# From the ninth pair on, DMA transposes the third row block's probabilities as planes of half words; x and residual pages share one ring

## The chip, the cores and the metric

The kernel runs on one core of a Trainium2 chip. The metric is device time in microseconds of one launch. Engines: TensorE (PE, with weight loads listed as PEld), VectorE (DVE), ScalarE (ACT), GpSimd (POOL), and SyncE (SP), which issues almost all DMAs. Each engine runs its instructions in the order of its own queue; semaphores hold an instruction until what it reads has been written and what it overwrites has been read.

## The reference

Two stages. Attention, with B = 8, H = 8, S = 576, D = 64, masked by blocks of 64 positions; then a gated MLP on x, the attention output laid out as (B, S, 512):

```python
scores = scale * np.matmul(q, k.transpose(0, 1, 3, 2))
mask = block_i >= block_j                     # blocks of 64 positions
scores = np.where(mask, scores, -1000000000.0)
attn = np.exp(scores - np.max(scores, axis=-1, keepdims=True))
attn = attn / (np.sum(attn, axis=-1, keepdims=True) + 1e-09)
x = np.matmul(attn, v)                        # (B, H, S, D), then to (B, S, H*D)

h = gelu_tanh(x @ w_in)                       # 512 -> 1024
u, v = h[..., :512], h[..., 512:]
v_n = (v - mean(v)) / np.sqrt(var(v) + 1e-06) * g_ln
v_s = np.einsum('ts,bsd->btd', w_sg, v_n) + b_sg[None, :, None]
out = x + (u * v_s) @ w_out
```

All tensors are float32.

## The kernel before

**Work and slots.** A pair is one batch and two heads; there are 32, four to a batch. The main loop runs one *slot* for each pair n. It finishes pair n (transposes of its probabilities, product with v, normalisation) and makes the scores and probabilities of pair n+1; in the *holes* between these steps PE gets pieces of the MLP of an earlier batch. Slots 0 to 3 are `opening_slot`, 4 to 7 `middle_slot`, 8 to 31 `slot`. The pieces come from `work` in the order v, u, o of the batch before, s, so that the four slots of a batch differ: from slot 8 on the first has mostly v pieces (x @ w_in for the v half, `accv`), the second u pieces (`accu`), the third the eight o pieces (w_out and the residual sum, `acco`) along with the LayerNorm of v, the fourth s pieces (spatial product and gate, `accs`). They are called the v, u, o and s slot; slots 8 and 12 are v slots, 10 and 14 o slots.

**Precision.** A float32 product is made of three matmuls of split operands, hi and lo (`xh`, `xl`, `kh`, `kl`, ...). The transposes of the probabilities and their product with v are plain float32.

**One slot in order** (`slot`). Loads of v and of q, k for later pairs; `turn("A0")`, `turn("A1")`: four 128 x 128 transposes each by PE into a PSUM bank, copied to an SBUF page `pt`; holes; `turn("B0")`, `turn("B1")`; holes; `turn("C")`: the four blocks of the third row block `prob_119`, two of each head, copied by DVE into `ptC`; `turn_sums` (`pd`); holes; `Scores.first` of the next pair (scores `s`, masked maximum on DVE, exponent on ACT); `products` (`ob`, which reads all `pt` pages); `normalise`, which writes the page x and spills it to DRAM; `Scores.second`, whose last part is the third row block; `Values.inverse`, from pair 4 on `spread`: sums and their reciprocal on DVE, the 32 x 32 block transpose `rt`, a DMA of it to DRAM (`rows`), and two DMAs that spread the rows over the partitions (`rb`); `split_qk` on POOL; holes, with LayerNorm work of DVE in between. So the end of `rt` on DVE marks the end of a slot's attention work.

**What sets the order.** Through slot 7 all engines keep program order. From slot 8 on only PE does (`written.intersection_update("P")`); the instructions of DVE, ACT, POOL and SP are put in order by a scheduler when the program is built. Two kinds of DVE work keep their program order all the same: `bn_stats` (L659) and the centring (L665).

**Pages.** `pt` has five buffers, shared by `ptA`, `ptB`, `ptC`, the last part of v (`vt`) and, up to slot 10, the conversion of w_out (`tm`). The page x has a ring of two buffers ("x"), the residual `xr` another ring of two ("r"): the o pieces load a spilled x into `xr`, add `acco` to it, and store it to `out_T`. The tag `rx` serves only pairs 0 to 3.

The lines that the change and the prediction touch:

```python
KINDS = {"x": ("x", 2), "xr": ("r", 2), "xh": ("y", 5), "xl": ("z", 5)}
TE = {"A0": "a", "A1": "v", "B0": "a", "B1": "v", "C": "v"}
"C": [(0, 2, 0), (0, 2, 1), (1, 2, 0), (1, 2, 1)],     # head, row block, column block
```

Of the kernel before, what the change touches and what calls it, by code (L numbers as in the profile page):

```python
# [9 lines left out]
F32 = mybir.dt.float32  # L10
F32R = mybir.dt.float32r
BF16 = mybir.dt.bfloat16
U32 = mybir.dt.uint32
AF = mybir.ActivationFunctionType
ALU = mybir.AluOpType
# [5 lines left out]
def kernel(  # L21
# [14 lines left out]
    P = 128  # L36
    BLK = 64
# [24 lines left out]
    vector = Engine("V", nc.vector)  # L62
    scalar = Engine("A", nc.scalar)
    gpsimd = Engine("G", nc.gpsimd)
    tensor = Engine("P", nc.tensor)
    sync = Engine("S", nc.sync)

    cp = ctx.enter_context(tc.tile_pool(name="cp", bufs=1))
    sp = ctx.enter_context(tc.tile_pool(name="sp", bufs=1))
    dp = ctx.enter_context(tc.tile_pool(name="dp", bufs=2, space=DRAM))  # L70
    psum = ctx.enter_context(tc.tile_pool(name="psum", bufs=1, space=PSUM))

    KINDS = {"x": ("x", 2), "xr": ("r", 2), "xh": ("y", 5), "xl": ("z", 5)}
    KINDS.update({n: ("a", 9) for n in ("vv", "vh", "vl")})
    KINDS.update({n: ("b", 12) for n in ("u", "gh", "gl", "w")})

    def page(dtype, n, name):
        tag, bufs = KINDS.get(name, KINDS["w"])
        return sp.tile([P, n], dtype, tag=tag, name=name, bufs=bufs)

    def bank(name):
        return psum.tile([P, 512], F32, tag="bank", name=name, bufs=8)
# [10 lines left out]
    def copy(e, dst, src):  # L93
        f = {"v": vector.tensor_copy, "a": scalar.copy, "g": gpsimd.tensor_copy}[e]
        return f(dst, src)
# [28 lines left out]
    def split_qk(n):  # L124
        out = []
        for x, t in zip(raw.pop(n), "qk"):
            hi = sp.tile([P, S], F32R, tag=t + "h", name=t + "h", bufs=1)
            lo = sp.tile([P, S], F32R, tag=t + "l", name=t + "l", bufs=1)
            if n:
                copy("g", hi, x)  # L130
                behind["G"] = gpsimd.tensor_tensor(lo, x, hi.bitcast(F32), op=ALU.subtract)
            out += [hi, lo]
        qk[n] = out
# [47 lines left out]
    MW = EXT[NT - 2]  # L181
    mask = cp.tile([P, MW], BF16, name="mask")
    gpsimd.memset(mask, 0.0)
# [12 lines left out]
    for s in (0, 1):  # L196
        t = cp.tile([P, NT - 1, 2 * D], F32, name=f"v_f{s}")
        d = cp.tile([P, NT, 2 * D], F32, name=f"v_d{s}")
        for a in (0, 1):
            r = slice(a * D, (a + 1) * D)  # L200
# [4 lines left out]
    prob = [[pairs[i][:, a * EXT[i] : (a + 1) * EXT[i]] for i in range(NT)] for a in (0, 1)]  # L205
# [39 lines left out]
    def load_weight(src, off, cols, dh, dl, name, size):  # L245

        parts = [(c, f) for f in range(0, cols, W) for c in range(NC)]
        for k in range(0, len(parts), size):
# [9 lines left out]
            if src.dtype == F32:  # L258
# [5 lines left out]
                continue  # L264
            words = [x.bitcast(U32).rearrange("p (n t) -> p n t", t=2) for x in raw]
            if size == 2:
                m = page(U32, size * W, name)
            else:
                tm = sp.tile([P, 2 * W], U32, tag="pt", name="tm", bufs=5)
                t, m = tm[:, :W], tm[:, W:]  # L270
# [8 lines left out]
            if size == 2:  # L279
                t = page(U32, size * W, name)  # L280
                y = bank("w").bitcast(U32)
            else:
# [180 lines left out]
    Q = H // 2  # L463
# [9 lines left out]
    class Values:  # L473
# [20 lines left out]
        def inverse(self):  # L494
# [9 lines left out]
                r.unsqueeze(2).broadcast_to([P, NT * 2, D]),  # L504
            )

        def spread(self):

            r = sums32[:, : 2 * NT]
            vector.tensor_scalar_add(  # L510
                r.rearrange("p (a i) -> p a i", a=2), self.sm.rearrange("p i a -> p a i"), 1e-9
            )
            vector.reciprocal(r, r)
            rt = sp.tile([P, 32], F32, tag="rt", name="rt", bufs=1)
            vector.transpose(rt, sums32)
            rows32 = dp.tile([32, P], F32, tag="rows", name="rows", bufs=2)
            sync.dma_start(rows32.rearrange("c (g p) -> g c p", g=P // 32), rt)
            while between:
                between.popleft()()
            rows = rows32[: 2 * NT, :].rearrange("(a i) p -> a (i p)", a=2)  # L520
            self.d = sp.tile([P, NT * BLK + S], F32, tag="rb", name="rb", bufs=1)
            rb = self.d[:, NT * BLK :]
            for a in (0, 1):
                sync.dma_start(
                    rb[a * D : (a + 1) * D, :], rows[a : a + 1, :S].broadcast_to([D, S])
                )
            self.rb = rb[:, : S - BLK]
            self.r0 = rb[:, S - BLK :]
# [68 lines left out]
    def run_side(k):  # L597

        while k > 0 and side and side[0][0] != "G":
            k -= 1  # L600
            side.popleft()[1]()
# [187 lines left out]
    def hole(k=1):  # L789

        while k > 0 and work:
            try:
                next(work[0])
                k -= 1
            except StopIteration:
                work.popleft()
# [64 lines left out]
    def slot(n, va):  # L861
        nx = n + 1 < N
        k = 3
        g = [int(x) for x in (FIRST if n // Q == 1 else PLAN)[n % Q]]
        if n + 1 < N:
            load_v(n + 1)
        if n + 2 < N:
            load_qk(n + 2)
        va.turn("A0")
        va.turn("A1")  # L870
        hole(g[0])
        run_side(k)
        split_pending()
        load_share(n, 0)
        va.turn("B0")
        va.turn("B1")
        hole(g[1])
        run_side(k)
        va.turn("C")
        va.turn_sums()  # L880
        hole(g[2])
        run_gelu()
        load_share(n, 1)
        if nx:
            nx = Scores(n + 1)
            nx.first()
        va.products()
        va.normalise()
        if nx:
            nx.second()  # L890
        load_share(n, 2)
        if n % Q == Q - 1:
            va.split()
        else:
            pending.append(va.split)
        nv = None
        if nx:
            nv = Values(n + 1, nx)
            nv.inverse()
        if n + 2 < N:  # L900
            split_qk(n + 2)
        load_share(n, 3)
        for _ in range(g[3]):
            hole()
            run_side(k)
        return nx, nv
# [55 lines left out]
    def middle_slot(n, va):  # L962

        script = SCRIPT[n]
        g = [int(x) for x in FIRST[n % Q]]
        load_qk(n + 2)
        load_v(n + 1)
        va.turn("A0")
        va.turn("A1")
        if n != 2 * Q - 2:  # L970
            split_pending()
        run_gelu()
        hole(g[0])
        script[0]()
        va.turn("B0")
        va.turn("B1")
        hole(g[1])
        script[1]()
        va.turn("C")
        va.turn_sums()  # L980
        hole(g[2])
        script[2]()
        nx = Scores(n + 1)
        nx.first()
        va.products()
        va.normalise()
        nx.second()
        if n % Q == Q - 1:
            va.split()
        else:  # L990
            pending.append(va.split)
        script[3]()
        nv = Values(n + 1, nx)
        nv.inverse()
        split_qk(n + 2)
        script[4]()
        hole(g[3])
        script[5]()
        return nx, nv
# [14 lines left out]
    va = Values(0, sc)  # L1014
    for n in range(N):
        if n == 2 * Q:
            written.intersection_update("P")
        sc, va = (opening_slot, middle_slot, slot)[min(n // Q, 2)](n, va)
# [51 lines left out]
```

## Time and profile before

| what | value |
|---|---|
| median of 3 runs | 735.6 us (735.31 to 735.82) |
| the profiled execution | 736.18 us, span 734.1 us, mean granted clock 0.997 |
| PE busy | 721.1 us (98%) in 6796 matmuls |
| DVE busy | 481.0 us (66%) |
| ACT busy | 397.6 us (54%) |
| POOL busy | 301.2 us (41%) |
| DMA | 78.75 MB, 107 GB/s over the span |
| `pC`, 128 transposes | 20.2 us busy, pipelined |
| `ptC` by DVE, 24 copies | 16.5 us busy |

Busy times are of one execution. A line such as "DVE ... x32 | 13.6, 468 | 0.6" reads: 32 instructions, 13.6 us together, 468 ns each, and 0.6 us in which the engine stood idle just before them, with what ended the wait. In a timeline the two numbers ahead are the start and the duration in us, and the bracket is the idle time before and its releaser. Matmuls overlap, so what a block of them holds of PE is the distance between starts. "SPq" is SP issuing a DMA; the duration is that of the issue, not of the transfer.

### The profile page before, as it was taken

Reading aid. Unit: us, or ns where it says so; the run is one execution under the profiler, and the core shown is the slowest. Engines: PE = TensorE matmul, PEld = TensorE weight load, DVE = VectorE, ACT = ScalarE, POOL = GpSimd, SP = SyncE. Lnnn points to the kernel's source line nnn. Section 1 sums busy time; section 2 is a strip of 40 time slices with the busy share of each in tenths; the row PEclk is TensorE's granted clock in tenths of the full one; section 3 lists DMA queues with packets and bytes.
Section 4 is the critical chain, followed back from the end, with each engine's and each line's share of the span. In section 5 each row is a group of like instructions: output and inputs, shape, how many; then the busy total and the mean of one; then the engine's idle time right before and its main releaser. Section 6 shows DMA issues by size and latency. Waiting matters only on the chain.

```text
span 734.1 us, 18266 instructions
## 1 busy us (share of the span) xinstructions
PE 721.1 (98%) x6796; PEld 674.9 (92%) x6796; DVE 481.0 (66%) x1489; ACT 397.6 (54%) x1021; POOL 301.2 (41%) x333
## 2 busy tenths in 40 slices
PE   8999989999999999999999999999999999999998
PEld 7888979899998999989999899998999989998997
DVE  6988976569864487635876459654696456841732
ACT  6996768287533854347543575346663376602500
POOL 5868844555341253522445223453234433321120
PEclk9999999999999999999999999999999999999999
DMA  5667434354441225322263133531336322230032
GB/s 165 186 170 224 122 106 132 90 144 125 123 138 59 82 88 166 111 68 74 87 186 106 41 89 100 168 93 41 91 99 169 90 64 83 83 98 1 17 114 97
DMA packets 92907, 78.75 MB, mean 107 GB/s; under 512 B 64530, under 2 KB 65170, under 8 KB 92820
## 3 DMA queue, kind: packets, MB, share of 16 engines
q1 hardware_dynamic: 92532, 77.30, 35.8%
q8 instruction: 54, 0.88, 0.5%
q14 instruction: 33, 0.27, 0.1%
q10 hardware_dynamic: 288, 0.30, 0.1%
HBM read 58.23 MB, written 19.33 MB: 106 GB/s over the span
## 4 chain that ended last, share of the span: by engine, by line
PE 71%; DVE 15%; ACT 5%; POOL 4%; issue 3%; DMA 0%; SPq 0%; DVEq 0%; ACTq 0%; POOLq 0%
PE accs L60 16%; PE accv L60 14%; PE acco L60 9%; PE s L60 8%; PE ob L60 8%; PE accu L60 7%; ACT prob L60 4%; POOL rs L60 3%; DVE prob L60 3%; DVE bs L659 3%; PE pB L60 2%; PE pA L60 2%; DVE vl L60 2%; PE pd L60 2%; PE pC L60 1%
## 5 line engine op out<-in xcount | busy, mean ns | idle before, releaser
L60 ACT ACTIVATE prob<-prob,negm 128x576 f32<-128x576 f32 (+3 forms) x320 | 176.4, 553 | 58.0 <-DVE negm L60 56.6
L60 DVE CUSTOM_DVE_ANT_0 prob<-s,mask 128x256 f32<-128x256 f32 (+3 forms) x320 | 119.4, 417 | 36.8 <-PE s L60 33.9
L60 POOL TENSOR_TENSOR xh<-x,xh 128x64 fp32r<-128x64 f32 x32 | 10.3, 323 | 195.7 <-DVE xh L60 114.0
L60 POOL TENSOR_TENSOR gl<-u,gh 128x288 fp32r<-128x288 f32 x64 | 52.0, 818 | 86.0 <-DVE gh L60 65.9
L60 PE MATMUL acco<-gh,wo_h 128*128 128x288 f32 x256 | 77.3, 302 | 3.2 <-DVE negm L60 3.2
L60 PE MATMUL accu<-xh,wi_h 128*128 128x288 f32 x256 | 78.6, 307 | 0.0
L60 PE MATMUL accs<-ws_h,vh 128*128 128x288 f32 x256 | 77.9, 304 | 0.0
L60 PE MATMUL accu<-xh,wi_l 128*128 128x288 f32 x256 | 75.9, 296 | 0.0
L60 PE MATMUL accu<-xl,wi_h 128*128 128x288 f32 x256 | 75.8, 296 | 0.0
L60 PE MATMUL acco<-gh,wo_l 128*128 128x288 f32 x256 | 75.4, 295 | 0.0
L60 PE MATMUL accs<-ws_l,vh 128*128 128x288 f32 x256 | 75.4, 295 | 0.0
L60 PE MATMUL accs<-ws_h,vl 128*128 128x288 f32 x256 | 75.4, 294 | 0.0
L60 PE MATMUL acco<-gl,wo_h 128*128 128x288 f32 x256 | 75.3, 294 | 0.0
L60 PE MATMUL s<-kh,qh 64*128 64x320 f32 (+4 forms) x384 | 66.2, 325 | 3.2 <-DVE negm L60 2.7
L60 PE MATMUL accv<-wi_h,xh 128*128 128x512 f32 x160 | 65.5, 410 | 0.0
L60 DVE TENSOR_TENSOR u<-accs,u 128x288 f32<-128x288 f32 x64 | 29.2, 456 | 52.5 <-PE accs L60 50.0
L60 PE MATMUL accv<-wi_l,xh 128*128 128x512 f32 x160 | 63.1, 394 | 0.0
L60 PE MATMUL s<-kh,ql 64*128 64x320 f32 (+4 forms) x384 | 60.7, 304 | 0.0
L60 ACT ACTIVATION_READ_ACCUMULATOR prob<-prob,negm 128x1 f32 x320 | 60.0, 187 | 0.0
L60 PE MATMUL s<-kl,qh 64*128 64x320 f32 (+4 forms) x384 | 58.9, 301 | 0.0
L60 ACT COPY vv<-accv 128x512 f32<-128x512 f32 x32 | 18.6, 582 | 68.3 <-PE accv L60 68.3
L60 PEld LDWEIGHTS s<-kh,qh 64*128 64x128 f32 x384 | 38.3, 187 | 15.6 <-issue 9.1
(123 smaller groups left out, 2025.8 us busy)
## 6 DMA issues: line engine op xcount, KB each, us to landing
spill<-x SPq DMA_DIRECT2D x32, 288.0 KB
xr<-spill SPq DMA_DIRECT2D x32, 288.0 KB
out_T<-xr SPq DMA_DIRECT2D x32, 288.0 KB
q_f<-in_qT SPq DMA_DIRECT2D x31, 288.0 KB
k_f<-in_kT SPq DMA_DIRECT2D x31, 288.0 KB
rb<-rows SPq DMA_DIRECT2D x56, 144.0 KB
v_f<-in_v SPq DMA_DIRECT2D x32, 128.0 KB
v_d<-in_v SPq DMA_DIRECT2D x64, 64.0 KB
```

What stands on the lines that cost most here:

```text
L60: return lambda *a, **k: pin(method(*a, **k), self.letter)
L659: tc.keep_in_program_order(nc.vector.bn_stats(bs[:rows, :], x))
```

## The change

For pairs 8 to 31 the four PE transposes of `turn("C")` and DVE's copy out of PSUM go. In their place the new method `flip`, called right behind `inverse` in `slot` (for pair 8 in slot 7), views the float32 probabilities as pairs of half words: two POOL copies, one for each head, sort them into a plane of low and a plane of high half words (`halves`, 128 x 1024 of 16 bits, 256 KB); one transposing DMA on SP's queue turns its eight 128 x 128 blocks (`flipped`); one DVE copy of 1024 half words per partition joins the planes into float32 again, in `ptC`. The page x and the residual get one common ring of three buffers in place of two rings of two. Pairs 0 to 7 keep `turn("C")`.

```diff
-    KINDS = {"x": ("x", 2), "xr": ("r", 2), "xh": ("y", 5), "xl": ("z", 5)}
+    KINDS = {"x": ("x", 3), "xr": ("x", 3), "xh": ("y", 5), "xl": ("z", 5)}
...
+        def flip(self):
+
+            i = 2
+            halves = sp.tile([P, 2 * 2 * i * P], U16, tag="rx", name="halves", bufs=1)
+            sides = halves.rearrange("p (t a n) -> p t a n", t=2, a=2)
+            for a in (0, 1):
+                x = prob[a][i][:, a * BLK : a * BLK + i * P].bitcast(U16)
+                gpsimd.tensor_copy(sides[:, :, a, :], x.rearrange("p (n t) -> p t n", t=2))
+            flipped = sp.tile([P, 2 * 2 * i * P], U16, tag="flipped", name="flipped", bufs=1)
+            sync.dma_start_transpose(flipped.rearrange("p (m q) -> p m q", q=P), halves)
+            pt = sp.tile([P, 512], F32, tag="pt", name="ptC", bufs=5)
+            vector.tensor_copy(
+                pt.bitcast(U16).rearrange("p (n t) -> p t n", t=2),
+                flipped.rearrange("p (t n) -> p t n", t=2),
+            )
+            for a in (0, 1):
+                for j in range(i):
+                    c = (a * i + (i - 1 - j if a else j)) * P
+                    self.pt[a, i, j] = pt[:, c : c + P]
+
...
@@ slot
-        va.turn("C")
         va.turn_sums()
...
             nv.inverse()
+            nv.flip()
...
@@ middle_slot
         nv.inverse()
         split_qk(n + 2)
+        if n == 2 * Q - 1:
+            nv.flip()
```

On PE the order is otherwise the same. On DVE and SP the scheduler puts the work of a slot in another order. DVE at the start of slot 14, an o slot (530 us in the trace of before; `bs`, `stats` and `vv` are LayerNorm, `pA` and `pB` the PSUM banks of the transposes), before:

```order
L60 STREAM_TRANSPOSE rt<-sums_99 128x32
L659 BN_STATS bs<-vv 128x6
L60 BN_AGGR stats<-bs 128x2
L659 BN_STATS bs<-vv 128x6
L60 BN_AGGR stats<-bs 128x2
L659 BN_STATS bs<-vv 128x6
L60 CAST xh<-x 128x576
L60 BN_AGGR stats<-bs 128x2
L659 BN_STATS bs<-vv 128x6
L60 BN_AGGR stats<-bs 128x2
L659 BN_STATS bs<-vv 64x6
L60 COPY ptA_4146<-pA_4145 128x512
```

and with the change:

```order
L61 STREAM_TRANSPOSE rt<-sums_99 128x32
L61 CAST xh<-x 128x576
L61 TENSOR_TENSOR xr<-acco,xr 128x288 x2
L61 COPY ptC<-flipped 128x2x512
L680 BN_STATS bs<-vv 128x6
L61 COPY ptA_4153<-pA_4152 128x512
L61 COPY ptB_4216<-pB_4215 128x512
L61 TENSOR_TENSOR xr<-acco,xr 128x288
L61 BN_AGGR stats<-bs 128x2
L680 BN_STATS bs<-vv 128x6
```

The copy of `flipped` stands fourth, ahead of all five moments, of `ptA` and of `ptB`; before, `ptC` stood behind `ptB` and the centring. Two residual sums moved ahead of the moments. In v and u slots the copy stands directly behind `rt` with nothing between, in s slots behind two or three pairs of gate products (`u<-accs`, `gh<-u`).

SP at the same place, before (`xr_4152` and `xr_4168` are the first two residual pages of the o slot, loaded some twelve issues or more ahead of this):

```order
L60 DMA spill_4001<-x_3998 128x576
L60 DMA v_f1_113<-in_v 64x4x64 x2
L60 DMA v_d1_114<-in_v 64x4x64
L60 DMA rows_4031<-rt_4029 4x32x32
L60 DMA rb_4033<-rows_4031 64x576 x2
L60 DMA k_f_4135<-in_kT 128x576
L60 DMA q_f_4134<-in_qT 128x576
L60 DMA out_T<-xr_4152 128x576
L60 DMA xr_4388<-spill_1846 128x576
L60 DMA out_T<-xr_4168 128x576
```

and with the change:

```order
L61 DMA spill_4001<-x_3998 128x576
L61 DMA v_f1_113<-in_v 64x4x64 x2
L61 DMA v_d1_114<-in_v 64x4x64
L61 DMA xr_4159<-spill_1281 128x576
L61 DMA xr_4175<-spill_1577 128x576
L61 DMA rows_4031<-rt_4029 4x32x32
L61 DMA rb_4033<-rows_4031 64x576 x2
L61 DMA k_f_4142<-in_kT 128x576
L61 DMA_TRANSPOSE flipped_4039<-halves_4036 128x8x128
L61 DMA q_f_4141<-in_qT 128x576
L61 DMA out_T<-xr_4159 128x576
L61 DMA out_T<-xr_4175 128x576
```

The transpose stands behind `rows`, both `rb` and the load of k; in v and u slots it stands right behind `rb`. The two residual loads that ran far ahead are now issued just before `rows`, since the common ring has no buffer for them earlier.

More of the change, by code (lines that the diff above doesn't have):

```diff
@@ L12 @@
 BF16 = mybir.dt.bfloat16
+U16 = mybir.dt.uint16
 U32 = mybir.dt.uint32
```

## Prediction

> **What bounds the kernel now.** I read the busy times first, then the chain of waits that ended last, then the stretches between the ends of neighbouring `rt` transposes on VectorE (DVE), because that instruction closes a slot and the new copy is put right behind it.
>
> ```profile
> span 734.1 us, 18266 instructions
> PE 721.1 (98%) x6796; PEld 674.9 (92%) x6796; DVE 481.0 (66%) x1489; ACT 397.6 (54%) x1021; POOL 301.2 (41%) x333
> PE 71%; DVE 15%; ACT 5%; POOL 4%; issue 3%; DMA 0%; SPq 0%; DVEq 0%; ACTq 0%; POOLq 0%
> ```
>
> TensorE (PE) is busy for 98% of the span and is 71% of the chain; DVE at 66% looks free. By stretches (slots 8 to 11, then 12 to 15 of a later batch: v, u, o, s; columns: window, length, then the busy time of PE, weight loads, DVE, ScalarE (ACT), GpSimd (POOL), the granted clock, the DMA share) it is not free everywhere:
>
> ```profile
> 130.73:155.69 24.96, 24.96 (x206) 21.77 (x205) 16.68 (x50) 11.78 (x31) 12.98 (x17) 1.00 0.32 88
> 155.69:173.84 18.15, 18.15 (x193) 17.64 (x192) 13.02 (x47) 14.96 (x40) 8.70 (x13) 1.00 0.51 148
> 173.84:198.46 24.62, 24.39 (x243) 23.83 (x242) 23.53 (x63) 15.93 (x36) 12.38 (x15) 1.00 0.46 139
> 485.27:510.77 25.50, 25.50 (x209) 22.30 (x209) 12.20 (x39) 10.85 (x29) 10.84 (x12) 1.00 0.22 65
> 510.77:530.01 19.24, 19.24 (x203) 18.73 (x202) 9.85 (x35) 14.02 (x36) 4.93 (x5) 1.00 0.31 86
> 530.01:554.78 24.77, 23.99 (x235) 23.12 (x235) 22.56 (x62) 15.51 (x35) 10.76 (x10) 1.00 0.36 105
> 554.78:574.50 19.72, 19.72 (x206) 19.21 (x205) 12.93 (x46) 7.42 (x23) 7.26 (x10) 1.00 0.55 153
> ```
>
> In the v, u and s slots PE has no idle time and DVE has 7 to 13 us. In the o slot (530.01 to 554.78) DVE is busy for 22.56 of 24.77 us: only 2.2 us are idle, and PE loses 0.8. Slot 10 (173.84) is tighter still, 1.1 us. DVE is a second bound, once in each batch of four slots. A wait put on DVE there has no room.
>
> **What the change takes from PE.** Per slot from the ninth pair on, four transposes go. What they hold of PE is the step from their start to the next block's:
>
> ```profile
> 140.16 0.60 PE L60 MATMUL pC<-ident,prob 128*128 128x128 f32 x4
> 140.59 0.71 PE L60 MATMUL pd<-ident,prob 128*128 128x128 f32 x5
> ```
>
> That is 0.43 us a slot (140.59 − 140.16), and 24 × 0.43 = 10.3 us if PE bound every one of the 24 slots.
>
> **What it adds on other engines.** The trace has neither half-word copies nor a transposing DMA; the nearest rows are these:
>
> ```profile
> L60 POOL CAST kh<-k_f 128x576 fp32r<-128x576 f32 x31 | 20.8, 670 | 75.0 <-PE s L60 75.0
> L60 POOL TENSOR_TENSOR kl<-k_f,kh 128x576 fp32r<-128x576 f32 x31 | 45.1, 1455 | 0.7
> L60 DVE COPY ptC<-pC 128x512 f32<-128x512 f32 x24 | 16.5, 687 | 20.7 <-PE pC L60 19.4 <-POOL wo_l L60 1.3
> L60 DVE CAST xh<-x 128x576 fp32r<-128x576 f32 x29 | 13.6, 468 | 0.6
> L60 DVE SCALAR_TENSOR_TENSOR vl<-vv,rs,vh 128x512 fp32r<-128x512 f32 x32 | 23.7, 747 | 6.6 <-ACT vh L60 6.3
> 528.05 1.43 POOL L60 TENSOR_TENSOR ql<-q_f,qh 128x576 fp32r<-128x576 f32 x1
> ```
>
> POOL: two copies of 512 half words, 0.60 us each by elements from the cast (670/576), 1.29 by the two-input `kl` (1455/576). POOL's last split of q and k ends at 529.5 in the o slot and SP can issue the transpose at 533.9 (below), so either end is hidden; the copies would have to take 2.2 us each to be felt. DVE: the old copy out of PSUM (0.69) becomes one of 1024 half words from SBUF: 0.83 by the cast, 1.37 by the old copy, 1.5 by vl. I take 1.1, so +0.4 on DVE a slot, nothing in v, u and s slots, all of it in o slots.
>
> **Where the copy stands, and what it waits for.** By the order of the changed program `ptC<-flipped` is on DVE directly behind `rt`, in the o slot behind one `xh` cast and two `xr` sums, and the LayerNorm moments, `ptA`, `ptB`, the softmax maxima and the `vl` products are all behind it. DVE takes its queue in order, so all that waits until the transposed words have landed: PE's next products then wait for `ptA`, `ptB` and for the score banks that the maxima free, ACT for the scaled LayerNorm rows. Before, this was the work that filled the start of the slot (DVE, then SP):
>
> ```profile
> 529.80 0.21 DVE L60 STREAM_TRANSPOSE rt<-sums 128x32 f32<-128x32 f32 x1
> 529.93 0.65 DVE L659 BATCH_NORM_STATS2 bs<-vv 128x6 f32<-128x512 f32 x1
> 532.09 0.45 DVE L60 CAST xh<-x 128x576 fp32r<-128x576 f32 x1
> 534.59 3.37 DVE L665 SCALAR_TENSOR_TENSOR vv<-vv,stats,g_bc 128x512 f32<-128x512 f32 x5
> 537.88 0.81 DVE L60 TENSOR_TENSOR xr<-acco,xr 128x288 f32<-128x288 f32 x2
> 554.70 1.14 DVE L60 TENSOR_TENSOR xr<-acco,xr 128x288 f32<-128x288 f32 x3
> ```
>
> ```profile
> 530.04 0.57 SPq L60 DMA_DIRECT2D rows<-rt  x1
> 532.06 1.13 SPq L60 DMA_DIRECT2D rb<-rows  x2
> 533.28 0.54 SPq L60 DMA_DIRECT2D k_f<-in_kT  x1
> 533.91 0.38 SPq L60 DMA_DIRECT2D q_f<-in_qT  x1
> ```
>
> The transpose takes the place of the `q_f` load, so it is issued 3.9 us after the end of `rt` (533.91 − 530.01): `rb` waits 2.0 us for the 16 KB of `rows` to land, then two `rb` and one `k_f` are issued. In v and u slots it comes right behind `rb`, at 3.3 us (533.28). In s slots two or three pairs of gate products stand ahead of the copy and come only as fast as PE makes them, so the wait is covered there.
>
> **How long the transpose takes** from issue to landing is the unknown. The nearest rows are plain DMAs: 2.0 us for `rows` (16 KB), and for 288 KB the residual's load at the end and in a busier place:
>
> ```profile
> 725.30 2.03 SPq L60 DMA_DIRECT2D xr<-spill  x2
> 728.30 0.82 DVE L60 TENSOR_TENSOR xr<-acco,xr 128x288 f32<-128x288 f32 x2 [3.53 <-DMA xr<-spill]
> 697.73 4.04 SPq L60 DMA_DIRECT2D xr<-spill  x2
> 702.20 0.82 DVE L60 TENSOR_TENSOR xr<-acco,xr 128x288 f32<-128x288 f32 x2 [5.01 <-DMA xr<-spill]
> DMA packets 92907, 78.75 MB, mean 107 GB/s; under 512 B 64530, under 2 KB 65170, under 8 KB 92820
> q1 hardware_dynamic: 92532, 77.30, 35.8%
> ```
>
> DVE waited for them until 3.0 and 4.5 us after the issue. A mean packet costs 0.358 × 16 × 734.1 / 92532 = 45 ns of one engine. If the transpose writes rows of 128 half words it has 1024 of them: 46 us on one engine, 2.9 on all 16, plus the 2.0 that a small one needs, about 4.9. I take 4.5, with 2.0 as the lower end and 9 (twice, for a read and a write that don't overlap) as the upper one. The Trainium skill ("VectorE: DVE Perf Modes", section The three transpose paths) puts one 128 × 128 block of two-byte words through the DMA crossbar at 1309 ns against 390 ns on TensorE; as an estimate from that page eight blocks one after another are 10.5 us, and no run here shows it.
>
> **The sum**, against the profiled execution (736.2 us around a span of 734.1; the runs shown have a median 0.6 lower).
>
> - o slot: DVE's work is 22.56 − 0.69 + 1.1 + 1.14, since three more `xr` sums are ordered into this window that before ran just behind it (the x3 row) = 24.1. Ahead of the copy are 0.45 + 0.81 = 1.26, behind it 22.85. New length 3.9 + 4.5 + 22.85 = 31.25 against 24.77: **+6.5**. The other three slots give 3 × 0.43 = 1.3 back: +5.2 a batch, five batches (slots 12 to 31), **+26.0**. In v and u slots the hold is 7.8, and 7.8 + 12.6 and 7.8 + 10.3 stay under 25.50 and 19.24.
>
> In the first batch DVE also converts w_out, in three steps for each of eight pieces:
>
> ```profile
> L60 DVE SCALAR_TENSOR_TENSOR tm<-xr,tm 128x256 uint32<-128x256 uint32 x8 | 5.0, 647 | 0.1
> L60 DVE TENSOR_SCALAR tm<-xr 128x256 uint32<-128x256 uint32 x8 | 4.0, 520 | 2.0 <-DMA xr<-in_w_out 2.0
> L60 DVE SCALAR_TENSOR_TENSOR tm<-tm 128x256 uint32<-128x256 uint32 x8 | 3.8, 489 | 0.5 <-ACT tm L60 0.4
> ```
>
> - These stand behind the copy too, with two first and second steps and one third step more in slot 10 (2 × 1.17 + 0.49 = 2.8) and one piece fewer in slot 9 (of its 1.66 I count 1.1, since part of such a mean is time shared with POOL). Slot 10: 3.9 + 4.5 + (23.53 − 0.69 + 1.1 + 1.14 + 2.8 − 0.45 = 27.4) = 35.8 against 24.62, +11.2. Slot 9: 7.8 + 12.3 = 20.1 against 18.15, +2.0. Slot 8: 8.4 + 17.1 = 25.5 against 24.96, +0.5. Slot 11, a PE-bound one: −0.4. Together **+13.3**.
> - The shared ring of three buffers for x and residual: two of a batch's four residual loads now wait until another one's result is stored, a load of some 3.0 behind a store. The sums of these stand late in DVE's order, so I put nothing; without that cover it is 3 to 6 us a batch at most, inside the range.
>
> 39.3 on top of 736.2 is 775.5 for a profiled execution, **775** for the median. With the transpose at 2.0 the same sum is 4.0 − 1.3 a batch and 8.7 − 1.3 at first: +21, 757; with 3.0 it is +28, 763. With 6.5 us: 8.5 + 0.8 − 0.9 a batch (u slots begin to count) and +19 at first: +61, 797. With 9: 11.0 + 3.3 − 0.9 a batch, +27 at first: +94, 829.
>
> **Rivals.** *A quick transpose* (under 3 us, 25%). SP's `rows` speaks for it, the loaded 288 KB against it. Even one that lands at once leaves DVE over its room, since 3.9 us pass before it is issued: 757 to 763, say 759. The Trainium skill's page "Advanced Engine Details and Errata" (section X-Bar Transpose (TRN2)) says that transposing DMAs of this chip are as fast as regular ones; by that rule the plain rows above hold for it, 2.0 to 4.5 us, and the time is this case's or the forecast's.
>
> *A slow transpose* (over 6.5 us, 22%): its blocks go one after another, or it queues behind the `k_f` load issued just ahead of it. For it: it moves two-byte words, which no DMA of this trace does. Then u slots, and from 9.6 us on v slots (25.50 − 3.3 − 12.6), lose as well: 797 to some 860, 829 at 9 us. The same sum by the skill's 10.5 us would be some 855.
>
> *DVE's wait costs nothing* (8%): the copy finds its data there, and only PE's 10.3 us are left: 736 − 10 = **726**. For it: PE is 98% busy and 71% of the chain. Its place is the o slot and its price is whether the transposed words land within 24.77 − 22.85 = 1.9 us of `rt`; from there on each further microsecond costs one in each batch. Against it: SP can't even issue it before 3.9 us, unless `rows` no longer holds SP up. If the o slots alone stayed as they are, it would be 736 − 18 × 0.43 = 728.
>
> **How the numbers follow.** Forecast (3 to 6.5 us for the transpose) 45%, 775, own range 763 to 797; quick 25%; slow 22%; no cost 8%. A measurement of this kernel tells 0.2% (1.5 us) from no change. Faster 0.07; the same 0.02, as only a balance of gain and hold would give it; slower 0.91. The range leaves out the no-cost case and the slow transposes beyond some 9 us, and goes 7 us below the quick sum, because waits that DVE has anyway (its 2.2 idle us in an o slot) can overlap with the hold: 750 to 835.
>
> **What would show it.** Right: in the changed profile DVE's largest new wait is `ptC` for the DMA `flipped<-halves`, 5 to 8 us in o slots; windows between `rt` ends grow there by about 6 and in slot 10 by 11; v, u and s windows shrink by 0.4; PE's busy share falls to about 92% with idle time released by DVE (`ptB`, `negm`, `vl`). The transpose's issue comes about 4 us behind `rt`, and the copy takes 0.8 to 1.5 us. Wrong: no such wait (then 726), the copy itself at several microseconds, POOL's half-word copies at over 2.2 us each so that SP waits for them, or waits of SP on the x ring ahead of `rows`.

## The result and the profile after

The changed kernel takes 782.6 us (median of 4 runs, 781.17 to 784.71) against 735.7 beside it: a ratio of 1.064, 95% interval 1.0615 to 1.0665. That is 46.9 us slower; 775 was forecast, 39 slower, with the transpose landing 4.5 us after its issue. The profiled execution took 781.2 us, with a span of 778.1, 44.0 more than before.

The page of the changed kernel: its span, the busy times, and the shares of the chain that ended last.

```profile
span 778.1 us, 18111 instructions
PE 732.7 (94%) x6700; PEld 680.5 (87%) x6700; DVE 485.9 (62%) x1489; ACT 396.1 (51%) x1021; POOL 333.8 (43%) x381
PE 59%; DVE 21%; DMA 5%; issue 5%; POOL 4%; ACT 3%; SPq 2%; DVEq 0%; ACTq 0%; POOLq 0%
```

DVE does the same work as before (485.9 us against 481.0) and is a larger part of the chain; DMA, 0% before, has 5%. PE has 96 matmuls fewer and is busy for 11.6 us *more*, which is explained below.

The stretches between the ends of `rt`, in the columns used before (window, length, busy time of PE, weight loads, DVE, ACT, POOL, granted clock, DMA share): slots 8 to 10, then the v, u, o and s slots 24 to 27.

```profile
130.10:156.78 26.68, 25.00 (x196) 20.78 (x195) 15.58 (x47) 10.99 (x30) 14.26 (x20) 1.00 0.37 96
156.78:178.04 21.26, 19.00 (x188) 17.71 (x187) 11.04 (x43) 14.84 (x40) 9.68 (x14) 1.00 0.45 131
178.04:213.45 35.41, 28.64 (x257) 26.56 (x256) 28.14 (x70) 16.82 (x38) 19.22 (x19) 0.97 0.43 123
519.43:542.89 23.46, 23.46 (x194) 20.42 (x193) 11.48 (x39) 9.93 (x28) 9.80 (x13) 1.00 0.32 81
542.89:561.48 18.59, 18.59 (x195) 17.91 (x194) 8.69 (x33) 14.29 (x37) 5.25 (x7) 1.00 0.36 100
561.48:596.59 35.11, 29.24 (x257) 27.66 (x256) 25.36 (x64) 16.54 (x37) 15.95 (x15) 0.95 0.45 134
596.59:616.01 19.42, 19.42 (x191) 18.91 (x190) 12.63 (x44) 6.84 (x22) 7.97 (x11) 0.91 0.30 81
```

Over the whole trace the 44.0 us come out like this. Slots 8 to 11 grew by 16.5 (103.27 against 86.78), slots 12 to 30 by 30.4, and what lies ahead of slot 8 and behind slot 30 shrank by 0.6 and 2.3. In slots 12 to 29 the o slot grew from 24.77 to between 32.8 and 35.1 (33.9 on average), the v slot shrank from 25.50 to 23.46, the u slot from 19.24 to 18.59, and the s slot from 19.72 to 19.4, but for slot 23, which takes 20.6. The last o slot, 30, grew from 23.55 to 31.0. The v slot's 2 us are no saving of their own: it holds 15 matmuls fewer and the o slot 22 more, so work of PE has moved from one window into another. The late copy below has 193 matmuls in its v slot as well, so it is not DVE's long wait that moved them out of it.

DVE and SP at the start of o slot 26, whose `rt` ends at 561.48 (start, duration, and in brackets the idle time before with its releaser):

```profile
561.27 0.21 DVE L61 STREAM_TRANSPOSE rt<-sums 128x32 f32<-128x32 f32 x1
563.42 1.12 DVE L61 CAST xh<-x 128x576 fp32r<-128x576 f32 x1 [1.94 <-PE accu L61]
567.06 0.46 DVE L61 TENSOR_TENSOR xr<-acco,xr 128x288 f32<-128x288 f32 x1 [2.52 <-PE acco L61]
568.65 0.46 DVE L61 TENSOR_TENSOR xr<-acco,xr 128x288 f32<-128x288 f32 x1 [1.13 <-PE acco L61]
573.15 0.76 DVE L61 COPY ptC<-flipped 128x1024 uint16<-128x1024 uint16 x1 [4.05 <-DMA flipped<-halves]
573.80 0.68 DVE L680 BATCH_NORM_STATS2 bs<-vv 128x6 f32<-128x512 f32 x1
```

```profile
560.77 1.08 SPq L61 DMA_DIRECT2D xr<-spill  x2
561.94 0.58 SPq L61 DMA_DIRECT2D rows<-rt  x1
565.44 1.14 SPq L61 DMA_DIRECT2D rb<-rows  x2
566.68 0.54 SPq L61 DMA_DIRECT2D k_f<-in_kT  x1
567.33 1.28 SPq L61 DMA_TRANSPOSE flipped<-halves  x1
```

The first of the LayerNorm moments, which before followed `rt` at once, comes 12.3 us behind it. In between DVE works for 2.8 us. SP issues the transpose 5.85 us behind `rt`, and the copy begins 5.8 us later.

The new operations, from the listing by tiles (durations in ns, min/median/max; the last line is the landing of the transpose after its issue, in us, which the trace has for six of the 24):

```profile
L61 POOL COPY halves<-prob x48: 602/620/1391, 133.1 to 683.3; 128x512 uint16<-128x512 uint16 x48
L61 SPq DMA_TRANSPOSE flipped<-halves x24: 1249/1279/1363, 134.8 to 684.7; - x24
L61 DVE COPY ptC<-flipped x24: 736/757/1265, 139.6 to 690.4; 128x1024 uint16<-128x1024 uint16 x24
DMA to landing us min/median/max: 3.3/3.4/3.7
```

And from the list of waits, the new one and what it does to PE by way of `vl` (sum in us, times, longest):

```profile
DVE ptC L61 <- DMA flipped<-halves: 82.2, 19, 9.5
PE accs L61 <- DVE vl L61: 18.2, 8, 4.0
```

### The profile page after: what moved, and what is told of

It is laid out like the page before. It is cut to its first block, busy times and chain, and to the rows that moved or that the text cites. A ratio compares the mean times of both kernels' runs of the same rounds, so it can differ in the third digit from the quotient of the medians.

```text
span 778.1 us, 18111 instructions
## 1 busy us (share of the span) xinstructions
PE 732.7 (94%) x6700; PEld 680.5 (87%) x6700; DVE 485.9 (62%) x1489; ACT 396.1 (51%) x1021; POOL 333.8 (43%) x381
## 3 DMA queue, kind: packets, MB, share of 16 engines
q1 hardware_dynamic: 117876, 83.60, 38.4%
## 4 chain that ended last, share of the span: by engine, by line
PE 59%; DVE 21%; DMA 5%; issue 5%; POOL 4%; ACT 3%; SPq 2%; DVEq 0%; ACTq 0%; POOLq 0%
PE accs L61 15%; PE accv L61 12%; PE accu L61 8%; PE s L61 7%; PE ob L61 7%; DMA flipped<-halves 4%; DVE prob L61 4%; PE acco L61 4%; DVE vv L686 3%; DVE vl L61 3%; DVE bs L680 2%; ACT prob L61 2%; PE pB L61 2%; SPq L61 2%; DVE vn_t L61 2%
## 5 line engine op out<-in xcount | busy, mean ns | idle before, releaser
L61 PE MATMUL accs<-ws_h,vl 128*128 128x288 f32 x256 | 80.4, 314 | 18.3 <-DVE vl L61 18.2
L61 PE MATMUL acco<-gh,wo_h 128*128 128x288 f32 x256 | 80.2, 313 | 9.5 <-DVE x L61 9.3
L61 PE MATMUL accs<-ws_h,vh 128*128 128x288 f32 x256 | 81.8, 320 | 1.3 <-ACT vh L61 1.3
L61 PE MATMUL accs<-ws_l,vh 128*128 128x288 f32 x256 | 79.1, 309 | 0.0
L61 PE MATMUL acco<-gl,wo_h 128*128 128x288 f32 x256 | 77.5, 303 | 0.0
L61 PE MATMUL acco<-gh,wo_l 128*128 128x288 f32 x256 | 77.5, 303 | 0.0
L61 DVE COPY ptC<-flipped 128x1024 uint16<-128x1024 uint16 x24 | 18.6, 777 | 82.2 <-DMA flipped<-halves 82.2
L61 PEld LDWEIGHTS accs<-ws_h,vl 128*128 128x128 f32 x256 | 51.5, 201 | 20.6 <-DVE vl L61 20.3
L61 ACT COPY vv<-accv 128x512 f32<-128x512 f32 x32 | 18.6, 582 | 98.9 <-PE accv L61 98.9
L61 PEld LDWEIGHTS acco<-gh,wo_h 128*128 128x128 f32 x256 | 50.0, 195 | 12.2 <-DVE x L61 10.7
```

The source lines that it names most:

```text
L61: return lambda *a, **k: pin(method(*a, **k), self.letter)
```

## The experiments

**Theory**: the wait of `ptC<-flipped` stands at the head of DVE's queue, the LayerNorm moments, copies and maxima are behind it, and in o slots DVE has no room. **Rivals**: the shared ring costs; the added work on POOL and DVE or the transfers cost by contention; the words are too late for PE itself.

### One ring, nothing else

```diff
-    KINDS = {"x": ("x", 2), "xr": ("r", 2), ...
+    KINDS = {"x": ("x", 3), "xr": ("x", 3), ...      # on the kernel before
```

> The kernel before with one part of the change alone: x and residual share one ring of three pages; the transposes of the third row block stay on TensorE. Theory (the copy of the transposed words holds DVE's queue in the o slots): nothing of this is here, DVE's order is that of before, so 735.7 within 0.3%; at most one or two us a batch from residual loads that now wait for a page. Rival (the shared ring is what costs: residual pages arrive late): 760 or more, with DVE waiting for the DMA of xr in the o slots.

Measured: 735.6 us, ratio 1.0003 (0.999 to 1.0016). The ring alone costs nothing; the o slots are 24.77 as before. It does put two residual loads in front of `rows` here too, and `rb` comes 2.1 to 3.0 us behind `rt` (before 2.0 to 2.3), but no engine stands behind that.

### Without the transposing DMA

```diff
-            flipped = sp.tile([P, 2 * 2 * i * P], U16, tag="flipped", name="flipped", bufs=1)
-            sync.dma_start_transpose(flipped.rearrange("p (m q) -> p m q", q=P), halves)
+            flipped = halves
```

> The changed kernel without the transposing DMA: DVE's copy reads the two half-word planes directly, so the third row block's blocks are not transposed and the output is not the reference's. All of the change's work on POOL and DVE, its place in DVE's order and the ring stay. Theory (hold behind the DMA): the copy finds its data about 1 us behind rt, the o slots fall from 34 to some 24 to 26 us, slot 10 from 35 to 28, PE's 0.43 us a slot shows, the granted clock is back at 1.00: 730 to 742. Rival (the added work itself, POOL's and DVE's copies and their shared port, or the reordered DVE work, makes DVE the bound): 765 or more.

Measured: 744.9 us, ratio 1.0125 (1.0103 to 1.0147). So 37.7 of the 46.9 us hang on the DMA: its issue, its transfer and the wait for it. The added copies on POOL and DVE do not make the loss; that rival stood at 765 or more. But 9 us of loss are left, over the theory's 742: slots 8 to 11 are 10.9 us longer than before (97.69 against 86.78), slots 12 to 30 are 3.8 longer, and what lies around them is 5.7 shorter. The o and the s slot of a late batch:

```profile
538.20:568.01 29.81, 27.38 (x260) 26.30 (x259) 24.68 (x64) 16.10 (x37) 16.01 (x15) 1.00 0.45 137
568.01:585.55 17.54, 17.54 (x188) 17.02 (x188) 12.53 (x44) 6.83 (x22) 8.40 (x12) 1.00 0.31 94
```

In slots 14 to 26 the o slot is 3 to 5 us shorter than in the change and still 5 longer than before. Its copy starts 5.95 us behind `rt` in every o slot from 14 on though its data lie ready from 1.4 us on: `xr<-acco` stands ahead of it in DVE's queue, and PE's `acco` is not done sooner. DVE in slot 26, whose `rt` ends at 538.20:

```profile
543.78 0.46 DVE L61 TENSOR_TENSOR xr<-acco,xr 128x288 f32<-128x288 f32 x1 [2.50 <-PE acco L61]
544.15 0.76 DVE L61 COPY ptC<-halves 128x1024 uint16<-128x1024 uint16 x1
```

So the order itself is a part of the loss: what stands in front of the moments waits for PE, with or without a DMA. Of the 9.1 us by which the change lengthened these o slots on average, 5.0 are left without the DMA. Slot 10 shows it more strongly: it takes 32.65 us here, with its copy only 2.99 us behind `rt`, against 24.62 before and 35.41 in the change.

With this run the length of an o slot can be set against the start of its copy:

| kernel | o slot | copy starts behind `rt` | length | difference |
|---|---|---|---|---|
| without the DMA | 26 | 5.95 | 29.81 | 23.86 |
| the change | 14 | 10.87 | 34.31 | 23.44 |
| the change | 18 | 9.92 | 33.35 | 23.43 |
| the change | 22 | 9.38 | 32.82 | 23.44 |
| the change | 26 | 11.67 | 35.11 | 23.44 |

Whatever holds the copy, 23.4 to 23.9 us follow it in these slots. (In the last o slot of the change, slot 30, they are 22.4: 31.01 less 8.59.) That is the term "behind the copy" of the prediction (22.85).

### The copy later in DVE's queue

The copy is written where `turn("C")` was and held behind the copy of `ptB`; nothing else is edited. The scheduler then also puts the rest of DVE's order in the o slot back: the five moments follow `rt` at once, as before, and the first residual sums come behind them.

```diff
+            self.behind = copy("a" if which == "C" and self.n < 2 * Q else TE[which], pt, t)   # in turn
...
+        def join(self):                     # called in place of va.turn("C") in slot
+            pt = sp.tile([P, 512], F32, tag="pt", name="ptC", bufs=5)
+            with tc.issue_after(self.behind.ins):
+                vector.tensor_copy(pt..., self.flipped...)
```

> The changed kernel with only DVE's copy of the transposed words moved: it is written at the old place of the third turn and held behind the copies of ptB. POOL's copies, the DMA and the ring are unchanged. Theory (hold): the words have long landed when DVE gets there (ptB came 10 us behind rt before, the words land 9 to 12 us behind it), so nearly all of the loss goes and most of PE's 10.3 us shows: 726 to 734. Rival (the transposing DMA, its issue of 1.28 us on SP and POOL's copies cost by themselves, by contention): 750 or more.

Measured: 723.5 us, ratio 0.9839 (0.9824 to 0.9854): 59 us less than the change, 12 less than before, and under the theory's 726 to 734. The 59 us are the wait and the order together. The four late slots, and DVE in the o slot (`rt` ends at 521.74):

```profile
479.78:503.15 23.37, 23.37 (x193) 20.35 (x193) 11.62 (x39) 10.02 (x28) 9.81 (x13) 1.00 0.32 82
503.15:521.74 18.59, 18.59 (x196) 17.91 (x194) 8.81 (x34) 14.51 (x37) 5.27 (x7) 1.00 0.37 100
521.74:545.40 23.66, 23.66 (x236) 23.14 (x235) 22.40 (x62) 15.84 (x36) 12.68 (x13) 1.00 0.55 158
545.40:565.96 20.56, 20.56 (x212) 20.05 (x211) 14.05 (x48) 7.42 (x23) 10.37 (x14) 1.00 0.43 122
```

```profile
521.66 0.65 DVE L686 BATCH_NORM_STATS2 bs<-vv 128x6 f32<-128x512 f32 x1
530.89 0.67 DVE L61 COPY ptB<-pB 128x512 f32<-128x512 f32 x1
531.70 0.76 DVE L61 COPY ptC<-flipped 128x1024 uint16<-128x1024 uint16 x1
```

PE has no idle time in any of the four, and the clock is whole. The POOL copies, the transposing DMA and its 1.28 us of issue are all still there: in these slots they cost PE no time. The batch takes 86.2 us against 89.2 before, 3.0 less where 4 × 0.43 = 1.7 was PE's share; the rest is the o slot's 0.8 us of PE idle time, gone, and some 0.5 that no run explains.

### The wait on POOL's queue

```diff
-            vector.tensor_copy(
+            gpsimd.tensor_copy(
                 pt.bitcast(U16).rearrange("p (n t) -> p t n", t=2),
```

> The changed kernel with the copy that joins the half words run by POOL instead of DVE; DMA, its issue and the ring are as in the change. Theory (what costs is that DVE's queue stands behind the wait): the wait moves to POOL, which has room, DVE's moments follow rt at once, o slots fall to 24 to 26 us: 722 to 738, a little above the late copy because POOL's 1.2 us copy stands in front of the second half of rs. Rival (the words themselves come too late for PE's products): above 750, with PE waiting for ptC.

Measured: 734.0 us, ratio 0.997 (0.9955 to 0.9985). The wait is as long as in the change and stands on another engine (list of waits):

```profile
POOL ptC L61 <- DMA flipped<-halves: 86.2, 23, 6.8
```

The windows of slots 9 and 10 and of the o slot 18:

```profile
156.99:181.75 24.76, 21.78 (x190) 20.29 (x189) 12.74 (x41) 14.94 (x40) 11.27 (x15) 0.86 0.41 115
181.75:214.03 32.28, 29.49 (x258) 27.95 (x257) 25.35 (x69) 17.20 (x39) 18.29 (x20) 0.95 0.46 129
359.95:385.40 25.45, 25.45 (x251) 24.93 (x250) 23.24 (x62) 16.43 (x37) 14.00 (x16) 1.00 0.52 150
```

86 us of waiting on POOL against 82 on DVE, and 48.6 us less time. So it is the queue that waits that sets the price, and the words come soon enough for PE: from slot 12 on PE has no idle time, and the batch takes 86.2 us as with the late copy. (Here too the moments follow `rt` at once, so this run and the late copy take away the wait together with the order; only the run without the DMA tells the two apart.) What keeps this kernel from the late copy's 723 are slots 9 and 10, with 24.76 and 32.28 us against 20.85 and 25.48. POOL also splits w_out there; that this is the reason is argued, not shown.

### The transpose on ACT's queue

```diff
-            sync.dma_start_transpose(flipped.rearrange("p (m q) -> p m q", q=P), halves)
+            scalar.dma_start_transpose(flipped.rearrange("p (m q) -> p m q", q=P), halves)
```

> The changed kernel with the transposing DMA issued by ACT and not by SP, so that it no longer stands behind rows, rb and the k load. The copy stays where the change has it. Theory: the hold has two parts, 4 to 6 us until SP issues and 3.4 to 5.8 us from issue to landing; the first falls to about 1 us, so the o slots lose 3 to 5 of their 34 us and slot 10 as much; PE idles less and keeps its clock: 750 to 765, with the DVE wait for flipped still there. Rival (the transfer alone is the hold, SP's queue is not): within 1% of 782. ACT may lose 1.3 us a slot for the issue, hidden at 51% busy.

Measured: 804.3 us, ratio 1.094 (1.0912 to 1.0968): slower still, and neither side's number. The reason I had for 750 to 765, an issue about 1 us behind `rt`, did not come about. Behind `rt` of slot 18 (388.60) ACT still has three copies of `accu`, which wait for PE, and a table load in front of the DMA (timeline, then the slot's window):

```profile
390.14 0.40 ACT L61 COPY u<-accu 128x288 f32<-128x288 f32 x1 [1.20 <-PE accu L61]
391.73 0.40 ACT L61 COPY u<-accu 128x288 f32<-128x288 f32 x1 [1.19 <-PE accu L61]
392.14 1.28 ACT L61 ACT_TABLE_LOAD   x1
393.52 1.47 ACTq L61 DMA_TRANSPOSE flipped<-halves  x1
```

```profile
388.60:426.43 37.83, 30.21 (x256) 28.73 (x255) 25.77 (x65) 16.65 (x37) 16.54 (x15) 0.88 0.56 133
```

It is issued 4.92 us behind `rt`, 1 us ahead of SP's in the change, and in this slot the copy starts 9.07 us after the issue, at 13.99. The four late o slots 14, 18, 22 and 26 start their copies at 10.47, 13.99, 10.11 and 11.90 and take 34.30, 37.83, 33.96 and 35.73: 23.83 to 23.85 more each time. Of the 27 us by which the profiled span is longer than the change's, slots 8 to 11 hold 8.1, and slots 17 and 18 together 9.8. The run does not say what SP's queue is worth, but it draws the same line between hold and length over another 4 us. Why the transfer took up to 9 us here beside SP's loads is open.

### The residual loads behind the transpose

```diff
-            sync.dma_start_transpose(...)
+            behind["T"] = sync.dma_start_transpose(...)
...
-                sync.dma_start(x_r[mo], spill.pop((b, mo)))
+                with tc.issue_after(behind["T"].ins):
+                    sync.dma_start(x_r[mo], spill.pop((b, mo)))
```

> The changed kernel with one thing different: the loads of the residual pages are held behind the latest transposing DMA on SP's queue, so that none of them stands in front of rows in the o slots. So far the length of an o slot has been the start of DVE's copy behind rt plus 23.4 to 23.9 us, in three kernels; in the changed kernel the copy starts at 8.6 to 11.7 us, of which rows takes 2.9 to 3.5 us to land against 2.0 elsewhere. Theory (the common ring puts two loads of 288 KB in front of rows and this lengthens the hold): rb at 2.1 and the issue at 3.9 us behind rt, the copy at some 8, o slots at 31.5 instead of 34: 766 to 774. Rival (the hold is the transfer's own time, or the loads only change places and delay the transfer or the residual sums): within 1% of 782.

Measured: 779.0 us, ratio 1.0564 (1.0534 to 1.0594): a little under the change's 1.064, with the intervals apart. The time lies above the theory's 766 to 774 and inside the rival's 1% of 782. The hold did shrink as expected, though. In slot 14 `rb` comes 2.05 and the issue 3.91 us behind `rt`, the copy 7.72. The windows of slots 14 and 15:

```profile
279.25:310.86 31.61, 27.27 (x256) 26.04 (x254) 24.98 (x60) 16.53 (x37) 16.71 (x15) 0.96 0.40 120
310.86:331.78 20.92, 20.69 (x192) 19.69 (x192) 14.23 (x49) 6.83 (x22) 7.53 (x11) 0.89 0.41 120
```

The o slot is 2.7 us shorter than slot 14 of the change (34.31), with the same 23.9 behind the copy. The s slot then is 1.5 longer (19.40 there), with 0.2 us of PE idle time and 0.89 of the clock, and slots 8 to 11 together are 107.2 instead of 103.3. Over the five o slots from 14 on the copy starts 7.2 to 8.7 us behind `rt`, 8.0 on average, against 8.6 to 11.7 and 10.1 in the change. So the loads ahead of `rows` are worth 2.1 us of hold in an o slot on average, from 0.7 to 3.9. The five o slots are 9.5 us shorter together; the four s slots behind them give 5.7 of that back, and slots 8 to 11 another 4.0.

### The late copy with other orders on SP's queue

Three variants of the late copy. First the residual loads behind the transpose (the edit of the experiment above):

> The late copy (held behind ptB) with the residual loads held behind the transposing DMA as well. In the late-copy run DVE still waits 20 us in 13 places for the words, 1 to 2.5 us in o and s slots. Theory: with the words some 2 us earlier in o slots part of this goes: 720 to 723.5. Rival: the residual sums wait for their later loads and take it back: 723.5 to 728.

Measured: 742.2 us, ratio 1.0076 (1.006 to 1.0092). Second, `flip` called ahead of `inverse` and `rows` held behind the transpose:

```diff
-            nv.inverse()
-            nv.flip()
+            nv.flip()
+            nv.inverse()                     # in spread: rows under tc.issue_after(behind["T"].ins)
```

> The late copy with the transposing DMA ahead of rows on SP's queue (rows held behind it). The words land 2 to 3 us earlier, rb comes 1.5 to 2 us later, and rb is not read before the normalisation at the end of the next slot's products. Theory: the remaining waits for the words go, 718 to 722. Rival: rows or rb comes too late, or those waits were hidden: 723 to 728.

Measured: 733.8 us, ratio 0.9959 (0.9943 to 0.9974). Both lie above their theories and their rivals, and for one reason. From slot 12 on they take 86.2 to 86.3 us a batch, where the late copy takes 85.7 to 86.5: nothing was left to gain there, since PE is without idle time in most of these slots. In slots 8 to 11 they lose 18.6 and 8.8 us to it (110.9 and 101.0 against 92.2). There DVE waits for w_out (15.3 us in the first of them), whose pages are in the ring that now also holds x and the residual; that the new order on SP's queue keeps these pages longer is argued, not shown. Windows of slots 10 and 14 of the second:

```profile
178.23:207.71 29.48, 24.19 (x236) 23.21 (x234) 23.25 (x62) 14.20 (x34) 16.39 (x18) 1.00 0.52 144
273.80:297.22 23.42, 23.42 (x234) 22.91 (x233) 22.30 (x62) 15.85 (x36) 12.66 (x14) 1.00 0.56 158
```

Third, pairs 8 to 11 keep `turn("C")`, so that the DMA path begins behind the weights, once with `rows` first and once with the transpose first:

```diff
+        if n >= 12: va.join()                # in slot, in place of va.turn("C")
+        else: va.turn("C")
+            if n >= 11: nv.flip()
```

> The late copy, but pairs 8 to 11 keep their transposes on TensorE; the DMA path runs for pairs 12 to 31. In the late-copy run slots 8 to 11 take 92.2 us against 86.8 before, the five batches behind them 86.8 against 89.2. Theory (what is left of the loss sits in the first batch, where w_out is still converted and shares pages): these four slots come back to some 86.8, the other batches stay at 86.8: 723.5 - 5.4 = 718, between 716.5 and 720. Rival (the first batch is long for another reason, the ring or the page order): 722 to 724.

> As the run before, and the transposing DMA issued ahead of rows. In the run with both over all pairs the batches from slot 12 on took 86.2 us, against 86.8 with the late copy alone, and only slots 8 to 11 were longer (101 us). Theory: 718 - 5 x 0.6 = 715, between 713.5 and 717.5, the remaining waits for the words gone. Rival (the first batch's loss had nothing to do with the flips in it): 725 or more.

Measured: 721.2 us, ratio 0.9799 (0.9782 to 0.9815), and 720.4 us, ratio 0.98 (0.9776 to 0.9823). Both are the fastest of this study, 2% under the kernel before, and the two can't be told apart. The first four slots came back to 87.6 us in both, so the first batch's loss did come from the flips in it. Both are above their forecasts (718 and 715): in the late copy slot 8 began at 129.14, here at 130.50 and 132.90. I had subtracted a gain in slots 8 to 11 without counting what lies ahead of them, and for the second one a gain in later batches that is not there.

## Why the prediction was right, by its steps

**The bound.** That DVE is a second bound in o slots, and nowhere else from slot 12 on, held. In u slots DVE stood still for 6.6 to 7.0 us behind `rt`, and from slot 12 on they shrank all the same; in o slots each microsecond of the hold is a microsecond of the slot. Against what stands ahead of the prediction, the copy does not follow `rt` directly in the v slots from 12 on: three pairs of gate products run in between, and the wait is only 2.3 to 4.7 us.

**PE's gain.** The 0.43 us a slot are real but do not show where PE waits. The u slot shrank by 0.65.

**The added work.** POOL's copies took 0.62 us (0.60 taken) and were hidden but in slot 8, where the second ended 4.2 us behind `rt` and the issue came at 4.7. The DVE copy took 0.76 where 1.1 was taken. SP's issue of 1.28 us was not priced at all and stands inside the time from issue to copy. DVE's work in an o slot was 25.4 us where 24.1 was summed.

**The transfer.** From the issue to the copy it was 3.2 to 3.9 us in the v and u slots but two (4.7 and 5.8), and 3.4 to 5.8 in the o slots from 14 on, 4.5 on average: the value taken. The packets are close to the 1024 assumed, too: queue q1 has 117,876 in place of 92,532, which is 1056 more for each of the 24 transposes. The rule of the Trainium skill that transposing DMAs are as fast as regular ones ("Advanced Engine Details and Errata", X-Bar Transpose (TRN2)) fits, with 3.4 us for 256 KB from the trace beside 3.0 for a plain 288 KB. The prediction's estimate of 10.5 us for eight blocks one after another, from the Trainium skill ("VectorE: DVE Perf Modes", The three transpose paths), does not: the measurement decides, and the slow rival falls with it.

**The term that was mis-sized** is the hold in the o slot: 3.9 + 4.5 = 8.4 us behind `rt`, measured 8.6 to 11.7 (mean 10.1 of five). The transfer was right; SP's chain was not: the issue came 5.2 to 6.0 us behind `rt`, not 3.9. The order that I showed has two residual loads right ahead of `rows`, and I costed them at nothing. `rows` is issued 0.45 to 1.0 us behind `rt`, and `rb` comes at 3.5 to 4.1 us instead of 2.0; the experiment that moved the loads took `rb` back to 2.05 to 2.8. In slots 14 to 26 the mean hold is 10.5 us, and 10.5 + 22.85 gives 33.3 for an o slot; the mean of these four is 33.9.

**Errors that balance.** The four batches of slots 12 to 27 grew by 6.4 us each (from 89.25 to 95.66 on average) where 5.2 was summed. The o slot grew by 9.1 instead of 6.5, but the other three slots gave back 2.7 instead of 1.3, mostly in the v slot, whose 2 us the sum did not have. That the total came within 8 us of the forecast is in part luck.

**A wait that was not seen.** The sum counts the work ahead of the copy in an o slot as 1.26 us. But the `xh` cast and the residual sums wait for PE, and without the DMA the copy comes at 5.95. In the change this lies under the longer hold, so the sum does not show it; two signs do. DVE's wait at the copy is 1.0 to 4.1 us in the o slots from 14 on, where 5 to 8 was to be seen. And with the words ready at once, the kernel without the DMA takes 744.9 us, not some 726.

**The first batch** was 13.3 by the sum and is 16.5: slot 10 at the forecast length (35.8, measured 35.4), slots 8 and 9 longer by 1.2 each, slot 11 by 1.3 at a clock of 0.89. The 35.4 of slot 10 do not show that the wait makes them, since 32.65 are left without the DMA. The late copy, without this hold, has slots 8 and 9 long too (26.25 and 20.85), so it is not DVE's wait there. In them `ptA`, `ptB` and `tm` share pages that POOL frees behind its copies; that this is the cause is argued, not shown.

**What was missing: the clock.** PE is busy 23.6 us longer than with the late copy (732.7 against 709.1) for the same 6700 matmuls. In slot 26, rows of PE's timeline and then two windows (the third number from the end is the granted clock):

```profile
583.49 0.29 PE L61 MATMUL acco<-gh,wo_l 128*128 128x288 f32 x1
586.06 0.40 PE L61 MATMUL acco<-gh,wo_h 128*128 128x288 f32 x1 [2.28 <-DVE x L61]
586.91 0.45 PE L61 MATMUL acco<-gl,wo_h 128*128 128x288 f32 x1
587.15 0.45 PE L61 MATMUL acco<-gh,wo_l 128*128 128x288 f32 x1
590.09 0.29 PE L61 MATMUL acco<-gh,wo_h 128*128 128x288 f32 x1
590.23 0.29 PE L61 MATMUL acco<-gl,wo_h 128*128 128x288 f32 x1
```

```profile
583.00:586.00 3.00, 0.79 (x6) 0.55 (x5) 3.00 (x6) 1.33 (x2) 3.00 (x4) 1.00 0.29 62
586.00:589.00 3.00, 2.94 (x13) 2.94 (x14) 3.00 (x12) 2.29 (x6) 3.00 (x2) 0.57 0.46 150
```

After 2.28 us without work the matmuls follow each other at 0.24 us instead of 0.13 to 0.14, for 3.5 us. At the start of the s slot this happens again, behind PE's wait for `vl`. It costs the s slot what it had saved: 19.42 us at a clock of 0.91, where the run without the DMA did nearly the same matmuls (188 against 191) in 17.54 at 1.00. These 1.9 us are why three of the four s slots from 15 on shrank by 0.3 and not by 2.2; slot 23, at a clock of 0.86, even grew by 0.9. Over the four that is, as an estimate, 8 to 9 of the 46.9 us.

**The rivals.** Slow transpose: no. Quick transpose: no, the copy never began less than 3.2 us after the issue. No cost: its condition, the words within 1.9 us of `rt`, could not be met, and where they were ready (without the DMA) 9 us of loss were left. But it names the repair, since a copy that does not stand ahead of the moments does not need that. The 726 forecast for "only PE's gain" is close to what moving the copy gave (723.5).

## What to carry to other kernels

Of an instruction that waits for a DMA, price what is queued behind it on its engine, not its own wait: with 82 us of waiting at the head of DVE's queue the kernel took 782.6 us, with 86 us on POOL's 734.0, and with the copy behind the work that DVE had anyway 723.5. Look as well at what the program's order puts ahead of such an instruction, for it may wait too: without any DMA to wait for, the copy still came 5.95 us behind `rt`, and the o slots stayed 5 us longer than before. Look at the stage where the "free" engine is not free: DVE at 66% was full in one slot of four. And count every transfer that is issued ahead of a chain of small DMAs; two loads in front of `rows` made up some 2 of the 10 us of hold.

## What was not expected of the hardware

- A transposing DMA of 256 KB of half words, 128 x 1024, took SP 1.28 us to issue, against 0.54 for a plain load of 288 KB, and landed 3.3 to 3.7 us after its issue in the six cases of 24 for which the trace has the landing. Where DVE's copy waited for it in the change, the copy began 3.2 to 5.8 us after the issue.
- PE's clock fell to half for about 3.5 us after gaps of some 2 us (granted clock 0.50 from 586.5 to 589.8 us in the change): in the traces of the change and of five experiments, 26 of the 27 gaps of 1.9 us and more ahead of a run of matmuls of 288 columns were followed by it, and none of the seven of 1.0 to 1.4 us; two gaps of 0.9 and 1.5 us close behind one another were. (Gaps inside a slow stretch, and short ones within some us of a longer one, are not counted.) Ahead of other matmuls less was enough: in the trace of before, gaps of 1.30 and 0.24 us among the scores at 104.9 us were followed by a granted clock of 0.50 from 105.5 to 108.7. The Trainium skill ("TensorE: Matmul & The Clock Gate", Part 1: The HAM clock gate) has half rate after at least one idle window of about 3.4 us; the length of the slow stretch agrees with that window, the gap that suffices is shorter here.
